# Forgetting attention with a spectral mode mix: attention matmuls padded to 128 rows, score blocks of one bank interleaved over four buffers

## The chip, the cores and the metric

One core of a Trainium2 chip. The metric is the device time of one execution in microseconds, the median of several executions; lower is better.

## The reference, cut to what matters

```python
# q, k, v: 8 batches x 8 heads x 576 x 64;  f: 8 x 8 x 576;  float32 in and out
scores = scale * q @ k^T                                # per batch and head, 576 x 576
decay  = cum[:, :, :, None] - cum[:, :, None, :]        # cum = cumsum(log f)
attn   = softmax(where(causal, -1e9, scores + decay))
x      = (attn @ v) laid out as [8, 576, 512]
X      = rfft(x, axis=1)[:, :64]                        # 64 modes
Y      = complex product of X[:, m] with w_r[m], w_i[m] # 64 pairs of 512 x 512 weights
u      = x + irfft(Y);   out = u + relu(u @ w_ch)
```

## The kernel before

Four stages follow one another: setup; attention, batch by batch, with the discrete Fourier transform of each batch; the 64 modes, whose 512 KB weight loads follow one another; output. The change touches attention and what its buffers are. In it, heads are taken in pairs; `S` is 576 and its five blocks have 128, 128, 128, 128 and 64 rows (`SBLK`).

```python
def emit_loads_and_casts(b):
    # ... qf, kf, vf float32 staging tiles, one buffer each; 15 loads per batch ...
                nc.sync.dma_start(dst[:ns, sc, :, :], t_dram[b, :, sc*128 : sc*128+ns, :]...)
    # ... cast by VectorE to qb, kb, vaug (bf16); the last block has 64 rows ...

def emit_qk_pair(b, g):                       # two heads, 2g and 2g + 1
    for sc in range(NSB):
        ns = SBLK[sc]
        nc.tensor.transpose(QTp[:, sc*128 : sc*128+ns], qb[:ns, sc, 2*g : 2*g+2, :]..., ident_bf[:ns, :ns])
        nc.tensor.transpose(KTp[...],                   kb[:ns, sc, 2*g : 2*g+2, :]..., ident_bf[:ns, :ns])
    nc.vector.tensor_copy(QTs[:, :], QTp[:, :])         # [128 = two heads x 64, S]
    nc.vector.tensor_copy(KTs[:, :], KTp[:, :])
    for hp in range(2):
        bp = hp * 64
        for jb in range(NSB):
            pscore = psA.tile([128, S], F32, ...)       # two banks; psA has two buffers
            for c0 in range(0, wj, 512):
                nc.tensor.matmul(pscore[:Mj, c0 : c0+n],
                    lhsT=KTs[bp : bp+64, s0 : s0+Mj], rhs=QTs[bp : bp+64, ...])   # 64 rows
            nc.scalar.activation(et[:Mj, :wj], pscore[:Mj, :wj], ACT.Exp, bias=..., scale=scale)
            nc.vector.tensor_tensor(et[:Mj, :Mj], et[:Mj, :Mj], trimask[:Mj, :Mj], ALU.mult)

def emit_dft_group(b, eb):                    # a transform: 5 matmuls, the last of 64 rows
    # ... pd[:, :] += x_b[:ns, sc, ...]^T @ bas[:ns, sc, ...]
    nc.vector.tensor_copy(XT[:, eb, :, :, b], pd...)    # XT is [128, NEB, NM, 2, B]

for b in range(B):
    emit_loads_and_casts(b)
    for g in range(H // 2):
        emit_qk_pair(b, g)
        # ... then 4 tail tasks of the batch before: value products (pav) and transforms (pd) ...
```

The softmax here doesn't subtract the row's maximum and nothing guards it: scores larger than these inputs give would overflow.

Of the kernel before, what the change touches and what calls it, by code (L numbers as in the profile page):

```python
# [10 lines left out]
F32 = mybir.dt.float32  # L11
# [12 lines left out]
def kernel(  # L24
# [28 lines left out]
    XT = xpool.tile([128, NEB, NM, 2, B], BF16, name="XT")  # L53
# [24 lines left out]
    wch = const.tile([128, NEB, D], BF16, name="wch")  # L78

# [116 lines left out]
    with ExitStack() as actx:  # L196
# [6 lines left out]
            tc.tile_pool(name="psA", bufs=2, space=bass.MemoryType.PSUM)  # L203
# [9 lines left out]
        per_batch = {}  # L213

        def emit_loads_and_casts(b):
# [3 lines left out]
            for t_dram, dst in ((q, qf), (k, kf), (v, vf)):  # L219
                for sc in range(NSB):  # L220
                    ns = SBLK[sc]
                    nc.sync.dma_start(  # L222
                        dst[:ns, sc, :, :],
                        t_dram[b, :, sc * 128 : sc * 128 + ns, :].rearrange(
                            "h p d -> p h d"
                        ),
                    )
            qb = qkbf.tile([128, NSB, H, Dh], BF16, tag="qb", name="qb")
            kb = qkbf.tile([128, NSB, H, Dh], BF16, tag="kb", name="kb")
            nc.vector.tensor_copy(qb[:, 0:4, :, :], qf[:, 0:4, :, :])  # L230
            nc.vector.tensor_copy(qb[:64, 4, :, :], qf[:64, 4, :, :])
            nc.vector.tensor_copy(kb[:, 0:4, :, :], kf[:, 0:4, :, :])  # L232
# [9 lines left out]
        def emit_qk_pair(b, g):  # L242
            st = per_batch[b]
            qb, kb = st["qb"], st["kb"]
            QTp = psT.tile([128, S], BF16, tag="tr", name="QTp")
            KTp = psT.tile([128, S], BF16, tag="tr", name="KTp")
            for sc in range(NSB):
                ns = SBLK[sc]
                nc.tensor.transpose(  # L249
                    QTp[:, sc * 128 : sc * 128 + ns],  # L250
                    qb[:ns, sc, 2 * g : 2 * g + 2, :].rearrange("p h d -> p (h d)"),
                    ident_bf[:ns, :ns],
                )
                nc.tensor.transpose(  # L254
                    KTp[:, sc * 128 : sc * 128 + ns],
                    kb[:ns, sc, 2 * g : 2 * g + 2, :].rearrange("p h d -> p (h d)"),
                    ident_bf[:ns, :ns],
                )
            QTs = qtkt.tile([128, S], BF16, tag="QTs", name="QTs")
            KTs = qtkt.tile([128, S], BF16, tag="KTs", name="KTs")  # L260
            nc.vector.tensor_copy(QTs[:, :], QTp[:, :])
            nc.vector.tensor_copy(KTs[:, :], KTp[:, :])
            for hp in range(2):
                h = 2 * g + hp
                bh = b * H + h
                bp = hp * 64
                for jb in range(NSB):
                    Mj = SBLK[jb]
                    s0 = jb * 128
                    wj = S - s0  # L270
                    pscore = psA.tile([128, S], F32, tag="sc", name="pscore")
                    for c0 in range(0, wj, 512):
                        n = min(512, wj - c0)
                        nc.tensor.matmul(  # L274
                            pscore[:Mj, c0 : c0 + n],
                            lhsT=KTs[bp : bp + 64, s0 : s0 + Mj],
                            rhs=QTs[bp : bp + 64, s0 + c0 : s0 + c0 + n],
# [3 lines left out]
                    et = epool.tile([128, wj], BF16, tag=f"e{jb}", name=f"et{jb}")  # L281
                    st["etiles"][(h, jb)] = et
                    nc.scalar.activation(  # L283
                        et[:Mj, :wj],
                        pscore[:Mj, :wj],
                        ACT.Exp,
                        bias=biasAll[:Mj, jb, bh : bh + 1],
                        scale=scale,
                    )
                    nc.vector.tensor_tensor(  # L290
                        et[:Mj, :Mj], et[:Mj, :Mj], trimask[:Mj, :Mj], ALU.mult
                    )
# [238 lines left out]
```

## Time and profile before

| | us |
|---|---|
| median of 6 runs first given | 716.82 (715.25 to 720.5) |
| median of all 16 runs of the comparison | 718.23 (715.25 to 720.5) |
| profiled span | 713.5 |
| to the first score matmul | 37.1 |
| attention, to the first mode matmul | 291.5 |
| modes / output | 318.5 / 66.4 |

Only one view is added here: the page's 40 equal slices of the span, each digit the busy share of an engine in tenths (9 is 90% or more); the last row is the TensorE clock, in tenths of full speed.

```profile
PE   0189999999998999899778752222222222227885
...
DVE  6356565656565656554222120000000000003454
ACT  2064646464545555461322320000000000003443
...
PEclk9999999999999999997999995555555555557998
```

Attention is slices 2 to 18, counted from 0: PE at eights and nines, VectorE (DVE) at fives and sixes, ScalarE (ACT) mostly at fours to sixes.

The clock entries of this trace hold two levels, 1.00 and 0.50, and all but the last are multiples of 3.41 us long; the shortest, at 323.93 us, is one such step. Below, warm is the level of 1.00 and cold that of 0.50; promotion is the change from cold to warm, demotion the change back; a window is one step of 3.41 us; a switch is where the next matmul has other rows or columns of the array.

### The profile page before, as it was taken

To read this page: it belongs to the slowest core of one execution; us is meant where nothing else is said; L and a number is where in the kernel's file an instruction comes from. 1 tells how busy PE (TensorE), PEld (TensorE's weight loads), DVE (VectorE), ACT (ScalarE), POOL (GpSimd) and SP (SyncE) were. 2 spreads that over 40 slices of the span, in tenths; PEclk is the share of its full clock that TensorE was granted. 3 is DMA by queue.
4 is the path that set the end of the run, shared out by engine and by line. 5 is a ranking of instruction groups with operands and counts; after the bars stand their busy time and mean duration, and the time that the engine had idled before them with its cause. 6 is when DMAs were issued, how large, how long until landed. Compare 5 with 4: busy or idle time off the path is not lost.

```text
span 713.5 us, 11166 instructions
## 1 busy us (share of the span) xinstructions
PE 452.9 (63%) x4412; PEld 253.4 (36%) x4428; DVE 264.5 (37%) x915; ACT 229.1 (32%) x478; POOL 98.5 (14%) x148
## 2 busy tenths in 40 slices
PE   0189999999998999899778752222222222227885
PEld 0035454545454544446444331111111111113332
DVE  6356565656565656554222120000000000003454
ACT  2064646464545555461322320000000000003443
POOL 3000000000000000002323232322323232210000
PEclk9999999999999999997999995555555555557998
DMA  9995536363645442004999999999999999993444
GB/s 194 212 213 108 114 71 129 68 131 70 116 85 112 88 94 41 1 1 76 204 207 206 207 206 206 206 206 206 206 206 206 207 206 207 206 207 84 158 164 148
DMA packets 186004, 106.78 MB, mean 150 GB/s; under 512 B 115232, under 2 KB 180768, under 8 KB 185952
## 3 DMA queue, kind: packets, MB, share of 16 engines
q0 software_dynamic: 67584, 67.12, 56.9%
q1 hardware_dynamic: 118368, 38.96, 25.7%
q8 instruction: 34, 0.56, 0.3%
q14 instruction: 18, 0.15, 0.1%
HBM read 163.73 MB, written 9.44 MB: 243 GB/s over the span
## 4 chain that ended last, share of the span: by engine, by line
DMA 44%; PE 37%; DVE 7%; ACT 5%; issue 4%; POOL 2%; SPq 1%; DVEq 0%; ACTq 0%; POOLq 0%
DMA wb<-in_moe_w_i_dram 38%; PE pscore L274 12%; PE pav L306 11%; ACT et L283 4%; DMA out_dram<-o_sb 4%; PE KTp L254 3%; PE pd L329 3%; PE QTp L249 3%; PE A L419 2%; POOL wb L409 2%; DVE o_sb L497 2%; DVE kb L232 2%; SPq L222 1%; DMA wch_f<-in_moe_w_ch_dram 1%; DMA kf<-in_k_dram 1%
## 5 line engine op out<-in xcount | busy, mean ns | idle before, releaser
L283 ACT ACTIVATE et<-pscore,biasAll 128x576 bf16<-128x576 f32 (+4 forms) x320 | 156.4, 524 | 142.1 <-PE pscore L274 137.2
L419 PE MATMUL A<-XT,wb 128*128 128x16 bf16 x2048 | 74.2, 174 | 189.8 <-DMA wb<-in_moe_w_r_dram 94.3
L274 PE MATMUL pscore<-QTs,KTs 64*128 64x512 bf16 (+5 forms) x384 | 128.3, 405 | 17.0 <-ACT et L283 14.5
L419 PEld LDWEIGHTS <-wb 128*128 128x128 bf16 x2048 | 63.2, 103 | 212.5 <-DMA wb<-in_moe_w_r_dram 106.7
L430 DVE TENSOR_TENSOR YT<-As 128x32 bf16<-128x32 f32 x64 | 19.2, 301 | 255.3 <-ACT As L427 255.3
L306 PE MATMUL pav<-vaug,et 128*128 128x65 bf16 (+2 forms) x960 | 97.0, 245 | 2.0 <-DVE x_all L315 0.2
L427 ACT COPY As<-A 128x128 f32<-128x128 f32 x64 | 17.0, 266 | 247.7 <-PE A L419 245.5
L290 DVE TENSOR_TENSOR et<-et,trimask 128x128 bf16<-128x128 bf16 (+1 forms) x320 | 64.6, 210 | 68.7 <-ACT et L283 66.3
L409 POOL DMA_DIRECT2D wb<-in_moe_w_r_dram x64 | 47.7, 745 | 282.8 <-PE A L419 271.2
L306 PEld LDWEIGHTS <-et 128*128 128x128 bf16 (+2 forms) x960 | 65.8, 130 | 57.7 <-issue 31.1
L274 PEld LDWEIGHTS <-KTs 64*128 64x128 bf16 (+1 forms) x384 | 38.2, 117 | 54.3 <-issue 40.8
L412 POOL DMA_DIRECT2D wb<-in_moe_w_i_dram x64 | 48.0, 750 | 1.8 <-issue 1.8
L398 PE MATMUL pxw<-wch,xT 128*128 128x512 bf16 (+1 forms) x148 | 42.4, 405 | 1.4 <-issue 0.6
L497 DVE SCALAR_TENSOR_TENSOR o_sb<-pz,u_sb 128x512 f32<-128x512 f32 (+1 forms) x40 | 27.5, 690 | 28.5 <-DMA out_dram<-o_sb 18.4
L239 POOL MEMSET vaug<- 128x40 bf16 x8 | 2.3, 282 | 250.3 <-PE pscore L274 119.2
L405 ACT CAST XW<-pxw 128x512 bf16<-128x512 f32 (+1 forms) x40 | 23.4, 585 | 38.7 <-PE pxw L398 36.4
L315 DVE TENSOR_TENSOR x_all<-pav,rcp 128x256 bf16<-128x256 f32 (+1 forms) x80 | 33.6, 420 | 0.6
L249 PE MATMUL QTp<-ident_bf,qb 128*128 128x128 bf16 (+1 forms) x160 | 26.1, 294 | 9.1 <-DVE qb L230 9.1
L254 PE MATMUL KTp<-ident_bf,kb 128*128 128x128 bf16 (+1 forms) x160 | 25.9, 292 | 7.5 <-DVE kb L232 7.5
L495 ACT CAST u_sb<-pu 128x512 bf16<-128x512 f32 (+1 forms) x40 | 23.4, 586 | 22.2 <-DVE o_sb L497 16.0
L329 PE MATMUL pd<-bas,x_all 128*128 128x128 bf16 (+1 forms) x160 | 24.5, 295 | 2.6 <-ACT et L283 2.3
L336 DVE CAST XT<-pd 128x128 bf16<-128x128 f32 x32 | 23.1, 730 | 4.9 <-PE pd L329 3.9
(90 smaller groups left out, 341.0 us busy)
## 6 DMA issues: line engine op xcount, KB each, us to landing
wb<-in_moe_w_r_dram POOLq DMA_DIRECT2D x64, 512.0 KB, 11.8
wb<-in_moe_w_i_dram POOLq DMA_DIRECT2D x64, 512.0 KB, 13.6
qf<-in_q_dram SPq DMA_DIRECT2D x32, 256.0 KB, 4.5
kf<-in_k_dram SPq DMA_DIRECT2D x32, 256.0 KB, 4.6
vf<-in_v_dram SPq DMA_DIRECT2D x32, 256.0 KB, 4.6
out_dram<-o_sb SPq DMA_DIRECT2D x32, 256.0 KB, 2.0
wch_f<-in_moe_w_ch_dram SPq DMA_DIRECT2D x1, 1024.0 KB, 5.8
qf<-in_q_dram SPq DMA_DIRECT2D x8, 128.0 KB, 4.5
```

The source lines that it names most:

```text
L249: nc.tensor.transpose(QTp[:, sc * 128 : sc * 128 + ns], qb[:ns, sc, 2 * g : 2 * g + 2, :].rearrange("p h d -> p (h d)"), ident_bf[:ns, :ns],)
L254: nc.tensor.transpose(KTp[:, sc * 128 : sc * 128 + ns], kb[:ns, sc, 2 * g : 2 * g + 2, :].rearrange("p h d -> p (h d)"), ident_bf[:ns, :ns],)
L274: nc.tensor.matmul(pscore[:Mj, c0 : c0 + n], lhsT=KTs[bp : bp + 64, s0 : s0 + Mj], rhs=QTs[bp : bp + 64, s0 + c0 : s0 + c0 + n], start=Tru ...
L283: nc.scalar.activation(et[:Mj, :wj], pscore[:Mj, :wj], ACT.Exp, bias=biasAll[:Mj, jb, bh : bh + 1], scale=scale,)
L290: nc.vector.tensor_tensor(et[:Mj, :Mj], et[:Mj, :Mj], trimask[:Mj, :Mj], ALU.mult)
L306: nc.tensor.matmul(pav[:Ms, hq, :], lhsT=et[:Mj, ccol : ccol + Ms], rhs=vaug[:Mj, h, jb, :], start=(jb == 0), stop=(jb == sb),)
L329: nc.tensor.matmul(pd[:, :], lhsT=x_b[:ns, sc, eb * 128 : (eb + 1) * 128], rhs=bas[:ns, sc, :, :].rearrange("p m ri -> p (m ri)"), start=( ...
L398: nc.tensor.matmul(pxw[:Ms, :], lhsT=xT[:, eb, sb * 128 : sb * 128 + Ms], rhs=wch[:, eb, :], start=(eb == 0), stop=(eb == NEB - 1),)
L409: nc.gpsimd.dma_start(wb[:, 0, :, :], moe_w_r[m].rearrange("(dc p) e -> p dc e", p=128))
L412: nc.gpsimd.dma_start(wb[:, 1, :, :], moe_w_i[m].rearrange("(dc p) e -> p dc e", p=128))
L419: nc.tensor.matmul(A[:, t, ebx, :], lhsT=wb[:, t, dc, ebx * 128 : (ebx + 1) * 128], rhs=XT[:, dc, m, :, :].rearrange("p ri b -> p (ri b)") ...
L497: nc.vector.scalar_tensor_tensor(o_sb[:Ms, :], pz[:Ms, :], 0.0, u_sb[:Ms, :], ALU.max, ALU.add)
```

## The change

Its intent: full use of the array's rows in attention, and scores that reach ScalarE without holes. It has these parts.

1. K of each head stands in its own copy `KTz` with zeros in the other head's 64 rows, so that a score matmul contracts over 128 rows; the last blocks of q, k and x are zero padded, so transposes and transforms have 128 rows.
2. Score blocks have at most 512 columns (one bank), in four buffers instead of two of two banks; the two heads of a pair alternate; the next pair's transposes and the last batch's tails are put between the score blocks.
3. `XT` has its modes contiguous, so the transform's eviction writes contiguous elements.
4. The v loads of batches 1 to 7 are issued on GpSimd's queue.

```diff
-    XT = xpool.tile([128, NEB, NM, 2, B], BF16, name="XT")
+    XT = xpool.tile([128, NEB, B, NM, 2], BF16, name="XT")
+    KTz = const.tile([128, 2, 2, S], BF16, name="KTz")
-            tc.tile_pool(name="psA", bufs=2, space=bass.MemoryType.PSUM)
+            tc.tile_pool(name="psA", bufs=4, space=bass.MemoryType.PSUM)
+        nc.vector.memset(KTz[64:128, :, 0, :], 0.0)
+        nc.vector.memset(KTz[0:64, :, 1, :], 0.0)
-                    nc.sync.dma_start(
+                    (nc.gpsimd if t_dram is v and b > 0 else nc.sync).dma_start(
+            nc.gpsimd.memset(qb[64:128, 4, :, :], 0.0)      # and kb, x_all
 # transposes: [:ns, ...] and ident_bf[:ns, :ns] become [:, ...] and ident_bf[:, :]
-            nc.vector.tensor_copy(KTs[:, :], KTp[:, :])
+                nc.vector.tensor_copy(KTz[0:64, slot, 0, :], KTp[0:64, :S])
+                nc.vector.tensor_copy(KTz[64:128, slot, 1, :], KTp[64:128, :S])
-            for hp in range(2):
-                for jb in range(NSB):
-                    pscore = psA.tile([128, S], F32, tag="sc", name="pscore")
+            for jb in range(NSB):
+                for c0 in range(0, wj, 512):
+                    for hp in range(2):
+                        pscore = psA.tile([128, 512], F32, tag="sc", name="pscore")
                         nc.tensor.matmul(
-                            lhsT=KTs[bp : bp + 64, s0 : s0 + Mj],
-                            rhs=QTs[bp : bp + 64, s0 + c0 : s0 + c0 + n],
+                            lhsT=KTz[:, g % 2, hp, s0 : s0 + Mj],
+                            rhs=QTs[:, s0 + c0 : s0 + c0 + n],
+                    # ... then the two activations and masks ...
+                if fillers:
+                    fillers.pop(0)()     # next pair's transposes, old tails
 # transform: x_b[:ns, ...], bas[:ns, ...] become x_b[:, ...], bas[:, ...]
-                XT[:, eb, :, :, b],
+                XT[:, eb, b, :, :],
 # mode matmul
-                            rhs=XT[:, dc, m, :, :].rearrange("p ri b -> p (ri b)"),
+                            rhs=_strided(XT[:, dc, 0, m, 0:1], [[1, 2], [NM * 2, B]]),
```

More of the change, by code (lines that the diff above doesn't have):

```diff
@@ L229, in emit_loads_and_casts @@
             kb = qkbf.tile([128, NSB, H, Dh], BF16, tag="kb", name="kb")
+            nc.gpsimd.memset(qb[64:128, 4, :, :], 0.0)
             nc.vector.tensor_copy(qb[:, 0:4, :, :], qf[:, 0:4, :, :])
             nc.vector.tensor_copy(qb[:64, 4, :, :], qf[:64, 4, :, :])
+            nc.gpsimd.memset(kb[64:128, 4, :, :], 0.0)
             nc.vector.tensor_copy(kb[:, 0:4, :, :], kf[:, 0:4, :, :])
@@ L240, in emit_loads_and_casts, with transpose_items @@
             per_batch[b] = dict(qb=qb, kb=kb, vaug=vaug, etiles={})
-        def emit_qk_pair(b, g):
+        def transpose_items(b, g):
             st = per_batch[b]
             qb, kb = st["qb"], st["kb"]
-            QTp = psT.tile([128, S], BF16, tag="tr", name="QTp")
-            KTp = psT.tile([128, S], BF16, tag="tr", name="KTp")
+            QTp = psT.tile([128, NSB * 128], BF16, tag="tr", name="QTp")
+            KTp = psT.tile([128, NSB * 128], BF16, tag="tr", name="KTp")
+            QTs = qtkt.tile([128, S], BF16, tag="QTs", name="QTs")
+            slot = g % 2
+            st[("QTs", g)] = QTs
+            items = []
@@ L247, in emit_qk_pair @@
             for sc in range(NSB):
                 ns = SBLK[sc]
-                nc.tensor.transpose(
-                    QTp[:, sc * 128 : sc * 128 + ns],
-                    qb[:ns, sc, 2 * g : 2 * g + 2, :].rearrange("p h d -> p (h d)"),
-                    ident_bf[:ns, :ns],
-                )
-                nc.tensor.transpose(
-                    KTp[:, sc * 128 : sc * 128 + ns],
-                    kb[:ns, sc, 2 * g : 2 * g + 2, :].rearrange("p h d -> p (h d)"),
-                    ident_bf[:ns, :ns],
-                )
@@ L259, in emit_qk_pair, with trq @@
-            QTs = qtkt.tile([128, S], BF16, tag="QTs", name="QTs")
-            KTs = qtkt.tile([128, S], BF16, tag="KTs", name="KTs")
-            nc.vector.tensor_copy(QTs[:, :], QTp[:, :])
-            nc.vector.tensor_copy(KTs[:, :], KTp[:, :])
+                def trq(sc=sc, ns=ns):
+                    nc.tensor.transpose(
+                        QTp[:, sc * 128 : sc * 128 + 128],
+                        qb[:, sc, 2 * g : 2 * g + 2, :].rearrange("p h d -> p (h d)"),
+                        ident_bf[:, :],
+                    )
@@ new lines, in trk, with evict @@
+                def trk(sc=sc, ns=ns):
+                    nc.tensor.transpose(
+                        KTp[:, sc * 128 : sc * 128 + 128],
+                        kb[:, sc, 2 * g : 2 * g + 2, :].rearrange("p h d -> p (h d)"),
+                        ident_bf[:, :],
+                    )
+                items.append(trq)
+                items.append(trk)
+            def evict():
+                nc.vector.tensor_copy(QTs[:, :], QTp[:, :S])
+                nc.vector.tensor_copy(KTz[0:64, slot, 0, :], KTp[0:64, :S])
+                nc.vector.tensor_copy(KTz[64:128, slot, 1, :], KTp[64:128, :S])
@@ L263, in emit_qk_pair @@
+            items.append(evict)
+            return items
+        def emit_qk_pair(b, g, fillers):
+            st = per_batch[b]
+            QTs = st[("QTs", g)]
+            ets = {}
             for hp in range(2):
                 h = 2 * g + hp
-                bh = b * H + h
-                bp = hp * 64
                 for jb in range(NSB):
-                    Mj = SBLK[jb]
-                    s0 = jb * 128
-                    wj = S - s0
-                    pscore = psA.tile([128, S], F32, tag="sc", name="pscore")
-                    for c0 in range(0, wj, 512):
-                        n = min(512, wj - c0)
+                    wj = S - jb * 128
+                    et = epool.tile([128, wj], BF16, tag=f"e{jb}", name=f"et{jb}")
+                    st["etiles"][(h, jb)] = et
+                    ets[(hp, jb)] = et
+            for jb in range(NSB):
+                Mj = SBLK[jb]
+                s0 = jb * 128
+                wj = S - s0
+                for c0 in range(0, wj, 512):
+                    n = min(512, wj - c0)
+                    pss = []
+                    for hp in range(2):
+                        pscore = psA.tile([128, 512], F32, tag="sc", name="pscore")
@@ L274, in emit_qk_pair @@
                         nc.tensor.matmul(
-                            pscore[:Mj, c0 : c0 + n],
-                            lhsT=KTs[bp : bp + 64, s0 : s0 + Mj],
-                            rhs=QTs[bp : bp + 64, s0 + c0 : s0 + c0 + n],
+                            pscore[:Mj, 0:n],
+                            lhsT=KTz[:, g % 2, hp, s0 : s0 + Mj],
+                            rhs=QTs[:, s0 + c0 : s0 + c0 + n],
                             start=True,
@@ L280, in emit_qk_pair @@
                         )
-                    et = epool.tile([128, wj], BF16, tag=f"e{jb}", name=f"et{jb}")
-                    st["etiles"][(h, jb)] = et
-                    nc.scalar.activation(
-                        et[:Mj, :wj],
-                        pscore[:Mj, :wj],
-                        ACT.Exp,
-                        bias=biasAll[:Mj, jb, bh : bh + 1],
-                        scale=scale,
-                    )
-                    nc.vector.tensor_tensor(
-                        et[:Mj, :Mj], et[:Mj, :Mj], trimask[:Mj, :Mj], ALU.mult
-                    )
+                        pss.append(pscore)
+                    for hp in range(2):
+                        h = 2 * g + hp
+                        bh = b * H + h
+                        et = ets[(hp, jb)]
+                        nc.scalar.activation(
+                            et[:Mj, c0 : c0 + n],
+                            pss[hp][:Mj, 0:n],
+                            ACT.Exp,
+                            bias=biasAll[:Mj, jb, bh : bh + 1],
+                            scale=scale,
+                        )
+                        if c0 == 0:
+                            nc.vector.tensor_tensor(
+                                et[:Mj, :Mj], et[:Mj, :Mj], trimask[:Mj, :Mj], ALU.mult
+                            )
+                if fillers:
+                    fillers.pop(0)()
         def emit_av_group(b, hh, sb):
@@ L325, in emit_dft_group @@
             x_b = x_all[:, b, :, :]
-            pd = psA.tile([128, 128], F32, tag="sc", name="pd")
+            pd = psA.tile([128, 512], F32, tag="sc", name="pd")
             for sc in range(NSB):
@@ L329, in emit_dft_group @@
                 nc.tensor.matmul(
-                    pd[:, :],
-                    lhsT=x_b[:ns, sc, eb * 128 : (eb + 1) * 128],
-                    rhs=bas[:ns, sc, :, :].rearrange("p m ri -> p (m ri)"),
+                    pd[:, 0:128],
+                    lhsT=x_b[:, sc, eb * 128 : (eb + 1) * 128],
+                    rhs=bas[:, sc, :, :].rearrange("p m ri -> p (m ri)"),
                     start=(sc == 0),
@@ L336, in emit_dft_group, with tail_items @@
             nc.vector.tensor_copy(
-                XT[:, eb, :, :, b],
-                pd[:, :].rearrange("p (m ri) -> p m ri", ri=2),
+                XT[:, eb, b, :, :],
+                pd[:, 0:128].rearrange("p (m ri) -> p m ri", ri=2),
             )
-        def tail_tasks(b):
+        def tail_items(b):
             tasks = []
@@ L344, in tail_tasks @@
                 for sb in range(NSB):
-                    tasks.append(("av", b, hh, sb))
+                    tasks.append(lambda b=b, hh=hh, sb=sb: emit_av_group(b, hh, sb))
             for eb in range(NEB):
-                tasks.append(("dft", b, eb))
+                tasks.append(lambda b=b, eb=eb: emit_dft_group(b, eb))
             return tasks
-        def run_task(t):
-            if t[0] == "av":
-                emit_av_group(t[1], t[2], t[3])
-            else:
-                emit_dft_group(t[1], t[2])
-        pending = []
-        for b in range(B):
-            emit_loads_and_casts(b)
-            for g in range(H // 2):
-                emit_qk_pair(b, g)
-                n_take = ((g + 1) * len(pending)) // (H // 2) if False else 4
-                for _ in range(min(len(pending), n_take)):
-                    run_task(pending.pop(0))
-            while pending:
-                run_task(pending.pop(0))
-            pending = tail_tasks(b)
-        while pending:
-            run_task(pending.pop(0))
+        nc.vector.memset(x_all[64:128, :, 4, :], 0.0)
+        pairs = [(b, g) for b in range(B) for g in range(H // 2)]
+        tails = []
+        for i, (b, g) in enumerate(pairs):
+            if i == 0:
+                emit_loads_and_casts(b)
+                for it in transpose_items(b, 0):
+                    it()
+            fillers = []
+            if i + 1 < len(pairs):
+                nb, ng = pairs[i + 1]
+                if ng == 0:
+                    emit_loads_and_casts(nb)
+                fillers.extend(transpose_items(nb, ng))
+            ntake = 4
+            for _ in range(min(ntake, len(tails))):
+                fillers.append(tails.pop(0))
+            emit_qk_pair(b, g, fillers)
+            for it in fillers:
+                it()
+            if g == H // 2 - 1:
+                while tails:
+                    tails.pop(0)()
+                tails = tail_items(b)
+        for it in tails:
+            it()
     with ExitStack() as bctx:
```

## The prediction

> **What bounds the kernel now.** I read the page's 40 slices first, then the chain, then the stretches of each stage. The chain's line by line shares:
>
> ```profile
> DMA wb<-in_moe_w_i_dram 38%; PE pscore L274 12%; PE pav L306 11%; ACT et L283 4%; DMA out_dram<-o_sb 4%; PE KTp L254 3%; PE pd L329 3%; PE QTp L249 3%; PE A L419 2%; POOL wb L409 2%; DVE o_sb L497 2%; DVE kb L232 2%; SPq L222 1%; DMA wch_f<-in_moe_w_ch_dram 1%; DMA kf<-in_k_dram 1%
> ```
>
> There are four stages: setup to the first score matmul at 37.1 us, attention to the first mode matmul at 328.6, the 64 modes (bound by the weight DMA, which holds 205 to 207 GB/s) to 648, output to 713. The change touches attention; a microsecond taken there moves the mode stage forward by a microsecond, because that stage needs the transforms of every batch and prefetches only three modes. Attention is 291.5 us, 36.5 per batch. Busy times of it, and of the mode stage (PE, PEld, DVE, ACT, POOL, clock, DMA share, GB/s):
>
> ```profile
> 72.00:288.00 216.00, 198.27 (x1342) 106.72 (x1342) 131.34 (x465) 117.20 (x240) 1.66 (x6) 1.00 0.48 92
> ...
> 430.00:645.00 215.00, 50.03 (x1344) 42.41 (x1344) 18.60 (x84) 11.17 (x42) 59.21 (x80) 0.50 1.24 205
> ```
>
> PE is busy 92% of attention, VectorE 61%, ScalarE 54%; ScalarE waits for PE (96.9 us), PE hardly for ScalarE (10.5):
>
> ```profile
> ACT et L283 <- PE pscore L274: 96.9, 85, 8.1
> ...
> PE pscore L274 <- ACT et L283: 10.5, 27, 0.5
> ```
>
> So attention is PE-bound. The clock of 1.00 above is not to be believed. The trace's clock records begin only at 323.93 us, with a grant of full speed; before that there is nothing, and the page prints nothing as full speed. The timeline across that moment:
>
> ```profile
> 320.59 1.59 PE L329 MATMUL pd<-bas,x_all 128*128 128x128 bf16 x10
> 322.12 1.56 PE L306 MATMUL pav<-vaug,et 128*128 128x65 bf16 x25
> 323.48 0.76 PE L329 MATMUL pd<-bas,x_all 128*128 128x128 bf16 x5
> 324.17 1.62 PE L306 MATMUL pav<-vaug,et 128*64 128x65 bf16 x20
> 325.73 1.05 PE L329 MATMUL pd<-bas,x_all 128*128 128x128 bf16 x10
> ```
>
> The same ten transform matmuls take 1.59 us before and 1.05 after. The groups by form say it again, first for 72 to 288, then for 324.2 to 327.5:
>
> ```profile
> L329 PE MATMUL pd<-bas,x_all 128*128 128x128 bf16 x96 | 14.5, 306 | 1.9 <-ACT et L283 1.9
> ```
>
> ```profile
> L329 PE MATMUL pd<-bas,x_all 128*128 128x128 bf16 x12 | 1.2, 224 | 0.4 <-DVE XT L336 0.4
> ```
>
> Start to start, the 25 value matmuls at 322.12 are (1.56-0.25)/24 = 55 ns apart for 65 columns, 0.84 ns a column; transform matmuls of 128 columns are 107 ns apart before 323.9 and 55 after. **All of attention runs at half clock.**
>
> I split the 216 us by start-to-start distance in the unmerged timeline (1,340 records). Streaming at 1.2 columns per ns: 137 us. Distance in excess of it where the next matmul has the same rows and columns of the array: 1 ns. Where rows or columns differ (64*128 after 128*128 and so on): 428 times, 130 ns each, 56 us. Long waits: 22 us. Per batch: 22.8 streaming, 9.3 switches, 3.7 waits.
>
> [...]
>
> **The change, part by part.**
>
> Padding to 128 rows (KTz, qb, kb, x_all). It removes every 64-row matmul of scores, transposes and transforms. Left are the column switches of the last score block (about 8 a batch) and of the value product's last block (18): 26 of 74. Saved at half clock: 48 x 130 ns = 6.2 us per batch. Streaming grows a little: 12,800 score + 7,800 value + 5,120 transpose + 2,560 transform columns = 28,280, 23.6 us cold, 11.8 warm.
>
> The clock. Weighting each window's streamed columns by rows/128, windows of this trace that promoted (outside transposes) had 0.63 to 0.87 of capacity, those of attention that did not at most 0.70; warm windows of 0.36 and more mostly held, 0.35 and less were demoted. This threshold is my estimate, from the trace's start times. With full rows a batch offers 23.3 us of weighted streaming in some 28: 0.8, so promotion. Warm, 11.7 in 25 is 0.47: mostly held, with cold windows now and then.
>
> ScalarE. The 576 activation is split into 512 and 64. By the rows below, +688-741+308 = 255 ns per head (688 interpolated), 2.0 us per batch: 19.5 becomes 21.5.
>
> ```profile
> L283 ACT ACTIVATE et<-pscore,biasAll 128x576 bf16<-128x576 f32 x48 | 35.6, 741 | 74.3 <-PE pscore L274 73.4 <-DVE x_all L315 0.8
> L283 ACT ACTIVATE et<-pscore,biasAll 128x448 bf16<-128x448 f32 x48 | 30.1, 627 | 0.0
> ...
> L283 ACT ACTIVATE et<-pscore,biasAll 64x64 bf16<-64x64 f32 x48 | 14.8, 308 | 5.6 <-PE pscore L274 4.0
> ```
>
> VectorE. The K eviction becomes two of 64 partitions, same 576 elements: 4 x 451 ns more. XT's new order lets the transform's eviction write 128 contiguous elements:[...] about 280, for 728: 4 x 450 ns less. Sum zero: 21.9 us per batch stays.
>
> ```profile
> L336 DVE CAST XT<-pd 128x128 bf16<-128x128 f32 x24 | 17.5, 728 | 3.7 <-PE pd L329 2.9
> ...
> L262 DVE COPY KTs<-KTp 128x576 bf16<-128x576 bf16 x23 | 10.4, 451 | 11.3 <-PE KTp L254 10.2 <-PE QTp L249 1.1
> ```
>
> Four one-bank score buffers for two of two banks, heads interleaved, next transposes and old tails as fillers: it shortens the 3.7 us of waits and lets PE feed ScalarE without long holes. The v loads on GpSimd take 5 of 15 issues (about 1.07 us each in the chain) off the sync queue; loads are hidden already (DMA share 0.48), so nothing, also at 25 us a batch (0.7). New memsets: x_all 4,096 elements and KTz 2 x 1,152[...]; +1 us. The mode matmul now reads its 16 columns in steps of 256 bytes; the stage uses PE 50 of 215 us, so nothing but at its ends.
>
> **Sum.** Warm, PE needs 11.8 + 26 x about 0.1 = 14 to 15 us per batch and the floor is VectorE 21.9 and ScalarE 21.5. Both near 87%[...]: 25 us. First batch, no tails, partly cold: 23. Last tails exposed, warm: 7. 23 + 7x25 + 7 = 205, plus 1 at the start: 291.5-206 = 85.5 saved, 716.8-85.5 = 631. I say 631.
>
> **Rivals.** (1) The clock stays cold. For it: before, 290 us of a 92% busy PE never promoted; transposes may not count as activity. Then PE stays the bound: 23.6 + 3.6 + 1.5 waits = 28.7; 24 + 7x28.7 + 10 = 235, so about 661. (2) VectorE and ScalarE pack to their floor: 22.3 a batch, 21 + 7x22.3 + 7 = 184, about 610. Against it: trimask and evictions wait on one another; the eviction of the next K stands in line on VectorE, and a late one stalls PE and ScalarE together. (3) It is given back in the mode stage by slow strided reads. Even 80 ns for 26 makes 32 matmuls 2.6 us, under the 5 us of DMA per mode; exposed at most at the first mode and the last, 4 us: 635. (4) The engines are bound by loads: needs 18 us of DMA per batch, under 25; little.
>
> **Range and chances.** Rivals 2 and 1 set the ends: 608 to 661. All of them are faster by over 7%, so faster 0.95; the rest is for a wrong schedule or for loads that hold up a batch.
>
> **What would show it.** Right: transform matmuls about 55 ns apart (mean near 224) in the middle of attention; clock records there; no 64*128 matmuls in scores, transposes, transforms; PE busy under 75%, VectorE and ScalarE near 85%; XT eviction near 280 ns; attention about 205 us; mode stage at 205 GB/s and as long as before. Wrong: matmuls still 107 ns apart (rival 1); XT eviction still 700; a mode stage longer by over 5 us; ScalarE waiting on DMA.

## The result, and the profile after

| | before | after |
|---|---|---|
| median us | 718.23 (16 runs) | 611.67 (609.53 to 612.76, 8 runs) |
| profiled span | 713.5 | 609.1 |
| start, to the first score matmul | 37.1 | 38.2 |
| first batch (its first exponential to that of the next) | 35.4 | 30.1 |
| batches 1 to 7, to the last exponential | 247.3 | 147.8 |
| last tails, to the first mode matmul | 8.1 | 7.0 |
| attention in all | 291.5 | 185.6 |
| modes | 318.5 | 318.4 |
| output | 66.4 | 66.9 |

(The three attention rows begin 0.7 us after the first score matmul, so they sum to 0.7 less than the whole.) The ratio is 0.852, 95% interval 0.8504 to 0.8536. Here and below a ratio compares the fast runs of the two kernels in the same rounds, so it is not quite the ratio of the medians quoted. The gain of 106 us is attention's; nothing was given back later. All outputs are right.

The slices of the kernel after, to be laid beside those of before:

```profile
PE   0156888988988998888772222222222222249885
...
DVE  8357899999999862123120000000000000015453
ACT  2047589988987832332330000000000000015443
...
PEclk9998699999999988898995555555555555559999
```

Attention now ends in slice 14, and VectorE stands at nines in it. This clock row is a record: the trace's clock entries begin at 40.4 us and show full speed to 57.4, half to 71.1 (the 6), then full speed without a break to 224.7. The chain that ended last has lost PE's share to the weight loads, which were as long before:

```profile
DMA wb<-in_moe_w_i_dram 45%; PE pav L343 6%; DMA out_dram<-o_sb 6%; PE pscore L305 4%; ACT et L317 4%; PE A L463 3%; POOL wb L453 3%; DVE o_sb L541 2%; DVE et L325 2%; DMA vf<-in_v_dram 2%; PE pxw L442 1%; DMA qf<-in_q_dram 1%; DVE x_all L352 1%; DVE vaug L241 1%; PE pd L366 1%
```

Busy times by stretch (PE, PEld, VectorE, ScalarE, GpSimd, clock, DMA share, GB/s): five whole batches, all of the steady part, and the mode stage.

```profile
89.30:197.20 107.90, 93.72 (x1085) 63.65 (x1084) 100.61 (x402) 92.39 (x241) 22.34 (x33) 1.00 0.77 144
...
72.00:217.00 145.00, 127.81 (x1485) 86.98 (x1482) 133.75 (x545) 126.03 (x330) 28.11 (x40) 1.00 0.68 128
235.00:542.00 307.00, 125.23 (x2194) 84.80 (x2204) 37.68 (x148) 37.26 (x97) 85.49 (x116) 0.62 1.23 205
```

VectorE is busy 93% of the five batches (100.61 of 107.90), ScalarE 86%, PE 87%. PE's figure counts each matmul from start to modelled end; by start-to-start distances PE's work is about 17.8 of 21.6 us per batch, so PE is no longer the bound. The modes move 205 GB/s, as before.

PE's groups by form, 72 to 217 us: the transform, 306 ns at half clock before, is

```profile
L366 PE MATMUL pd<-bas,x_all 128*128 128x128 bf16 x140 | 10.5, 219 | 0.7
```

That is the warm figure of the old kernel (224) all through attention, and the tile field shows no 64-row transform left. The groups of VectorE and of ScalarE, 89 to 197 us (count, busy us, mean ns, idle before):

```profile
L325 DVE TENSOR_TENSOR et<-et,trimask 128x128 bf16<-128x128 bf16 x160 | 29.5, 212 | 1.8 <-ACT et L317 0.8
...
L280 DVE COPY KTz<-KTp 64x576 bf16<-64x576 bf16 x20 | 9.2, 461 | 0.6
L279 DVE COPY KTz<-KTp 64x576 bf16<-64x576 bf16 x20 | 8.8, 441 | 0.0
...
L373 DVE CAST XT<-pd 128x128 bf16<-128x128 f32 x20 | 5.1, 280 | 0.2
```

```profile
L317 ACT ACTIVATE et<-pscore,biasAll 128x512 bf16<-128x512 f32 x41 | 26.1, 690 | 12.9 <-PE pscore L305 12.7 <-DVE et L325 0.2
L317 ACT ACTIVATE et<-pscore,biasAll 128x448 bf16<-128x448 f32 x40 | 23.7, 652 | 0.9 <-PE pscore L305 0.8
...
L317 ACT ACTIVATE et<-pscore,biasAll 128x64 bf16<-128x64 f32 x40 | 10.5, 325 | 0.0
```

The transform's eviction fell from 728 to 280 ns. Note 29.5 us of busy time for 160 masks of 212 ns, which would be 33.9: an instruction that follows at once starts before the one ahead has ended. This matters below. The waits of ScalarE and PE in the same stretch (total us, times, longest):

```profile
ACT et L317 <- PE pscore L305: 15.4, 21, 1.6
```

```profile
PE pscore L305 <- ACT et L317: 7.5, 29, 0.4
```

ScalarE's wait for PE fell from 96.9 us in 216 to 15.4 in 108. Last, the first batch, in its timeline:

```profile
57.97 1.23 DVE L241 CAST vaug<-vf 128x2048 bf16<-128x2048 f32 x1 [4.07 <-DMA vf<-in_v_dram]
...
68.98 1.27 ACT L317 ACTIVATE et<-pscore,biasAll 128x512 bf16<-128x512 f32 x2 [7.05 <-PE QTp L261]
```

VectorE sat idle 4 us for a load, the casts that stand behind it came late, and ScalarE idled 7 us before the second batch. This points to loads as the bound of the first batch; a run below tests it.

### The profile page after: what moved, and what is told of

It is laid out like the page before. It is cut to its first block, busy times and chain, and to the rows that moved or that the text cites. A ratio compares the mean times of both kernels' runs of the same rounds, so it can differ in the third digit from the quotient of the medians.

```text
span 609.1 us, 11331 instructions
## 1 busy us (share of the span) xinstructions
PE 353.6 (58%) x4411; PEld 224.7 (37%) x4428; DVE 256.0 (42%) x950; ACT 220.3 (36%) x542; POOL 138.6 (23%) x199
## 4 chain that ended last, share of the span: by engine, by line
DMA 53%; PE 17%; DVE 12%; ACT 4%; POOL 3%; issue 2%; SPq 0%; DVEq 0%; ACTq 0%
DMA wb<-in_moe_w_i_dram 45%; PE pav L343 6%; DMA out_dram<-o_sb 6%; PE pscore L305 4%; ACT et L317 4%; PE A L463 3%; POOL wb L453 3%; DVE o_sb L541 2%; DVE et L325 2%; DMA vf<-in_v_dram 2%; PE pxw L442 1%; DMA qf<-in_q_dram 1%; DVE x_all L352 1%; DVE vaug L241 1%; PE pd L366 1%
## 5 line engine op out<-in xcount | busy, mean ns | idle before, releaser
L317 ACT ACTIVATE et<-pscore,biasAll 128x320 bf16<-128x320 f32 (+5 forms) x384 | 147.7, 499 | 48.0 <-PE pscore L305 40.2
L474 DVE TENSOR_TENSOR YT<-As 128x32 bf16<-128x32 f32 x64 | 19.3, 302 | 254.9 <-ACT As L471 254.9
L305 PE MATMUL pscore<-QTs,KTz 128*128 128x512 bf16 (+1 forms) x383 | 89.6, 282 | 15.7 <-ACT et L317 11.6
L343 PE MATMUL pav<-vaug,et 128*128 128x65 bf16 (+2 forms) x960 | 66.4, 200 | 6.6 <-DVE x_all L352 5.9
L343 PEld LDWEIGHTS <-et 128*128 128x128 bf16 (+2 forms) x960 | 50.7, 103 | 29.2 <-DVE x_all L352 7.5
L305 PEld LDWEIGHTS <-KTz 128*128 128x128 bf16 (+1 forms) x384 | 35.8, 100 | 29.6 <-issue 13.2
L226 POOL DMA_DIRECT2D vf<-in_v_dram x35 | 30.4, 878 | 65.2 <-DMA qf<-in_q_dram 35.3
L539 ACT CAST u_sb<-pu 128x512 bf16<-128x512 f32 (+1 forms) x40 | 23.4, 586 | 22.1 <-DVE o_sb L541 13.8
L261 PE MATMUL QTp<-ident_bf,qb 128*128 128x128 bf16 x160 | 19.2, 233 | 13.9 <-DVE qb L235 11.2
L437 DVE COPY xT<-ptr 128x576 bf16<-128x576 bf16 x32 | 14.4, 464 | 22.8 <-PE ptr L432 22.7
L268 PE MATMUL KTp<-ident_bf,kb 128*128 128x128 bf16 x160 | 19.6, 231 | 6.1 <-DVE kb L238 5.2
L477 DVE TENSOR_TENSOR YT<-As 128x32 bf16<-128x32 f32 x64 | 21.6, 337 | 0.0
## 6 DMA issues: line engine op xcount, KB each, us to landing
wb<-in_moe_w_r_dram POOLq DMA_DIRECT2D x64, 512.0 KB, 11.7
```

The costliest lines, as they stand in the source:

```text
L226: (nc.gpsimd if t_dram is v and b > 0 else nc.sync).dma_start(dst[:ns, sc, :, :], t_dram[b, :, sc * 128 : sc * 128 + ns, :].rearrange("h p ...
L305: nc.tensor.matmul(pscore[:Mj, 0:n], lhsT=KTz[:, g % 2, hp, s0 : s0 + Mj], rhs=QTs[:, s0 + c0 : s0 + c0 + n], start=True, stop=True,)
L317: nc.scalar.activation(et[:Mj, c0 : c0 + n], pss[hp][:Mj, 0:n], ACT.Exp, bias=biasAll[:Mj, jb, bh : bh + 1], scale=scale,)
L343: nc.tensor.matmul(pav[:Ms, hq, :], lhsT=et[:Mj, ccol : ccol + Ms], rhs=vaug[:Mj, h, jb, :], start=(jb == 0), stop=(jb == sb),)
L539: nc.scalar.copy(u_sb[:Ms, :], pu[:Ms, :])
```

## The experiments

The main theory, **clock**: padding lets the array be granted full clock, and that is most of the gain. Its rival, **structure**: the four buffers, the interleave and the order take away waits, and padding saves only switches. Every ratio is to the kernel before in the same rounds.

### Padding alone

The kernel before with part 1 only: `KTz`, zero pads, 128-row transposes, scores and transforms; order, buffers, `XT` and load queues as before.

```diff
-                            lhsT=KTs[bp : bp + 64, s0 : s0 + Mj],
-                            rhs=QTs[bp : bp + 64, s0 + c0 : s0 + c0 + n],
+                            lhsT=KTz[:, g % 2, hp, s0 : s0 + Mj],
+                            rhs=QTs[:, s0 + c0 : s0 + c0 + n],
 # and the full-row transposes and transforms, as in the change
```

> The kernel before with the padding to 128 rows alone (scores, transposes, transforms); order of heads, score buffers, XT layout and v loads as before. Theory clock (full rows promote the clock, the rest matters little): transform matmuls 55 ns apart in attention, batches of 22 to 26 us, total 610 to 650. Rival switches[...]: clock stays at half, 36.5 - 6.2 = 30.3 us a batch, total about 667. Rival structure (fillers and four score buffers bring the gain): total about 690 to 710.

Measured: 681.1 us (675.31 to 682.91), ratio 0.9491 (0.9441 to 0.9541): a third of the gain. Its page's clock row:

```profile
PEclk9978787886565656858999955555555555557999
```

The clock swings: promoted, held for some windows, demoted again. By its records it is at full speed in 37% of attention, and a batch takes 29 to 35 us. So padding does get the clock promoted, as the clock theory has it, but alone it does not hold it. None of the three expectations was met exactly.

### Everything but padding

The kernel after with all padding removed (scores, transposes and transforms of 64 rows where they were so before; one K copy; no zero fills).

```diff
-                            lhsT=KTz[:, g % 2, hp, s0 : s0 + Mj],
-                            rhs=QTs[:, s0 + c0 : s0 + c0 + n],
+                            lhsT=KTz[hp*64 : hp*64+64, g % 2, s0 : s0 + Mj],
+                            rhs=QTs[hp*64 : hp*64+64, s0 + c0 : s0 + c0 + n],
 # and the ns-row transposes and transforms of the kernel before
```

> The changed kernel with all of its padding taken out (scores, transposes and transforms of 64 rows as before), but its order, buffers, XT layout and v loads kept. Clock: row-weighted activity stays under 0.70 of a cold window, no promotion, 32 to 36 us a batch, total 680 to 715. Structure: most of the gain stays, total 615 to 650.

Measured: 680.2 us, ratio 0.9494 (0.9469 to 0.9518). There is no clock record before 289.7 us, and the matmuls are spaced as at half clock: the nine below are (0.68-0.25)/8 = 54 ns apart for 65 columns.

```profile
136.72 0.68 PE L338 MATMUL pav<-vaug,et 128*128 128x65 bf16 x9
```

A batch takes 31.0 us. Counted by columns, PE streams 22.1 us per batch and waits 1.1 (3.7 before). But the 22.1 count some time twice: about six times a batch two score matmuls of 64 rows start 3 to 6 ns apart, which the kernel before never shows, and in all about 3 us of score columns per batch stream under one another. So the structure is worth about 36 us by itself, at half clock: of some 5.5 us per batch, about 2.5 are waits and 3 are this overlap of half-row matmuls, which padding gives up. The structure theory, which expected 615 to 650, falls.

By their ratios to some 717 us, padding alone takes 36 us, everything else 36, both 106. **The remaining 34 us come only with both**: padding supplies the activity, and the even feed holds the clock that it earns. (Since the overlap is lost with padding, this is the least that the two are worth to one another.)

### Scores of 64 rows, the rest padded

```diff
-                            lhsT=KTz[:, g % 2, hp, s0 : s0 + Mj],
-                            rhs=QTs[:, s0 + c0 : s0 + c0 + n],
+                            lhsT=KTz[hp*64 : hp*64+64, g % 2, s0 : s0 + Mj],
+                            rhs=QTs[hp*64 : hp*64+64, s0 + c0 : s0 + c0 + n],
```

> The changed kernel with only its score matmuls back at 64 rows (transposes and transforms stay padded). If the activity that promotes the clock is weighted by rows: 21,900 weighted columns a batch are 18.2 us of about 33 us, 0.55, mostly no promotion, total 670 to 700. If rows do not count, only streamed columns: 0.7 to 0.85 of the window, promotion, total 612 to 630. The two heads now follow one another in different halves of the rows and may overlap, which no theory above sizes.

Measured: 672.99 us, ratio 0.9381 (0.932 to 0.9441). The clock row:

```profile
PEclk9985555558555555679999755555555555558998
```

Full speed in 7% of attention only. **So it is the padding of the scores that the clock needs.** Why is less clear. The columns are the same as in the kernel after, but three things change with the rows of the scores: the rows themselves, the switches between 64 and 128 rows (130 ns each in the kernel before), and the overlap of the two heads (some nine pairs a batch start 3 to 6 ns apart). From the start times I counted, for each 3.4 us step of the clock records, the share of it in which columns streamed. Windows of this run that were not promoted had 0.50 to 1.03 with overlapping columns counted twice, 0.49 to 0.78 by time, and at most 0.74 weighted by rows/128. In the run of padding alone, promoted windows had 0.73 to 0.87 weighted (and some of up to 0.76 were not promoted), and 0.72 to 0.83 by time. At promotion, time and rows are thus too close to tell apart; the next run helps. The threshold, about 0.75, is an estimate from these counts, and not a sharp one: in the kernel after, the window that ended at 71.1 us was promoted at 0.67.

### A burst of full matmuls in the kernel before

16 dummy matmuls of 128 rows and 512 columns ahead of each batch, results unused; the other expectation was that promotion would last.

```diff
             for g in range(H // 2):
+                if g == 0:
+                    emit_burst()      # 16 x matmul(pb[:, 0:512], ident_bf, bas[:, 0:4])
                 emit_qk_pair(b, g)
```

> The kernel before with 16 more full matmuls of 512 columns in front of each batch (3.4 us of streaming warm, 6.8 cold, results unused). Clock: each burst fills a window and promotes; warm, weighted activity is about 0.34 to 0.4 of a window against a demotion level near 0.355, so attention is warm for some of each batch, and the kernel gets faster by added work: 620 to 700. Switches or structure: the burst only adds, 8 x 3.4 to 6.8 us, total 745 to 772.

Measured: 723.63 us, ratio 1.0101 (1.0072 to 1.013). Both expectations missed. The clock row of the page, and the bursts themselves as a group (72 to 288 us):

```profile
PEclk9855757575657575755899895555555555556999
```

```profile
L297 PE MATMUL pburst<-bas,ident_bf 128*128 128x512 bf16 x81 | 23.8, 457 | 0.0
```

Each burst brings some 10 us of full clock, then 27 us of half; the batch takes 37.6 us with the burst, 36.5 before. The burst nearly pays for itself, and the clock does not stay: promotion alone is not enough, the work after it must be dense enough to hold it.

These windows show that rows count. No matmuls overlap in them, yet in attention six of the seven that lost full speed had columns streaming for 0.41 to 0.48 of the time, by rows only 0.25 to 0.36; the kernel after held every window from 71.1 us on, down to 0.38.

### Two score buffers instead of four

```diff
-            tc.tile_pool(name="psA", bufs=4, space=bass.MemoryType.PSUM)
+            tc.tile_pool(name="psA", bufs=2, space=bass.MemoryType.PSUM)
```

> The changed kernel with two score buffers of one bank for four. If four buffers are what keeps PE's activity even enough to hold the clock: windows under 0.37 of capacity come back, the clock swings as in the padding-only kernel, total 640 to 690. If the order of heads and fillers holds it: 612 to 622.

Measured: 647.71 us, ratio 0.9026; 36 us more than the kernel after. A batch takes 26.8 us and the clock row has dips:

```profile
PEclk9987878899798996999889555555555555558999
```

Full speed in 79% of batches 1 to 6, against 98% with four buffers. In the runs with padding, windows at full speed with a weighted share of 0.38 or more held and those of 0.37 or less were demoted (estimates, from the same counts; the two overlap at the second digit). The kernel after has 0.38 to 0.72 in attention, and all windows from 71.1 us on held. The buffers are thus part of what makes the feed even. How much of the 36 us is the clock and how much is plain waiting was not separated.

### The old XT layout in the kernel after

```diff
-    XT = xpool.tile([128, NEB, B, NM, 2], BF16, name="XT")
+    XT = xpool.tile([128, NEB, NM, 2, B], BF16, name="XT")
 # eviction and mode matmul accordingly
```

> The changed kernel with only XT back in its old order: the transform's eviction writes 128 elements 16 bytes apart (about 730 to 790 ns for 280), and the mode matmul reads contiguous columns. If VectorE is the bound of attention (it is busy 20.4 of 22 us a batch): 4 x 0.45 to 0.5 = 1.8 to 2.0 us more a batch, total 624 to 628. If it is not, or if the strided read of the mode matmuls costs as much: 608 to 614.

Measured: 620.95 us (620.58 to 621.82), ratio 0.8658 (0.8637 to 0.8679): 9.3 us more than the kernel after. The eviction, and the busy times of its five batches 2 to 6:

```profile
L373 DVE CAST XT<-pd 128x128 bf16<-128x128 f32 x20 | 13.2, 791 | 0.2
```

```profile
90.70:204.70 114.00, 94.61 (x1084) 64.57 (x1082) 107.17 (x402) 94.13 (x241) 22.33 (x33) 0.97 0.72 135
```

VectorE's busy time rose by 1.3 us per batch (107.17 - 100.61 over 5) and the batch by 1.2 (22.8 for 21.6). It would have been 2.0 if each eviction's 511 extra ns stood alone; when the next instruction follows at once it started on average some 420 ns after the eviction's start, against 202 in the kernel after. The batch follows VectorE almost one for one. The rival is the clock, which fell to half twice here, for 3.4 us each; but batches 3 and 5, which have no such window, also took 23.0 to 23.1 us for 21.8. The mode stage is 318.4 us with either layout, though the mode matmul's median is 174 ns with the old one and 192 with the new. In the kernel after, its group on the page:

```profile
L463 PE MATMUL A<-XT,wb 128*128 128x16 bf16 x2048 | 82.4, 192 | 181.3 <-DMA wb<-in_moe_w_r_dram 92.3
```

PE waits for weights 181 us there. The slower read hides under the weight loads.

### The v loads back on the sync queue

```diff
-                    (nc.gpsimd if t_dram is v and b > 0 else nc.sync).dma_start(
+                    nc.sync.dma_start(
```

> The changed kernel with the v loads of all batches back on the sync queue. My prediction gave this part nothing: 608 to 616. Rival: 15 issues of about 1.1 us are 17 us of the queue per batch of 21 us, and loads come late: 618 to 640, with VectorE and PE waiting for loads after the first batch.

Measured: 623.4 us (622.9 to 624.3), ratio 0.8693 (0.8672 to 0.8713): 11.7 us more. Batches take 24 to 26 us, all but the last; the first takes 24.4, less than the 30.1 of the kernel after. The loads are not late: k of the batch shown was issued from 110.8 us on. At its boundary:

```profile
134.21 1.23 DVE L238 CAST kb<-kf 128x2048 bf16<-128x2048 f32 x1
...
137.94 0.69 ACT L317 ACTIVATE et<-pscore,biasAll 128x512 bf16<-128x512 f32 x1 [5.35 <-PE pscore L305]
```

The cast of K comes late among VectorE's instructions, at 134.21 us, behind the old batch's value tails; transposes, evictions and scores follow it, and ScalarE idles 5.35 us. The same place in the kernel after:

```profile
130.80 3.56 ACT L317 ACTIVATE et<-pscore,biasAll 128x512 bf16<-128x512 f32 x8 [1.56 <-PE pscore L305]
```

The two traces differ in the order of instructions on two engines: 416 of VectorE's 950 and about 1,430 of PE's 4,411 stand elsewhere, none of ScalarE's 542. So moving an issue from one queue to another changed the order in which the instructions were laid down, and most of the 11.7 us is put down to that order. A part is the clock: it fell to half for two windows in each of batches 3 and 6, which took 25.6 to 25.7 us where 1, 2, 4 and 5 took 24.7 to 24.9, so about 2 us. That the loads' own transfer took no part is argued from their times, not shown by a run.

### v cast in the load

v is loaded by GpSimd's queue straight into the bf16 tile, so VectorE has two casts fewer per batch.

```diff
-            vf = stg.tile([128, NSB, H, Dh], F32, tag="vf", name="vf")
+                nc.gpsimd.dma_start(vaug[:ns, :, sc, 0:Dh], v[b, :, sc*128 : sc*128+ns, :]...)
-            nc.vector.tensor_copy(vaug[:, :, 0:4, 0:Dh], vf[:, 0:4, :, :]...)   # and the last block
```

> The changed kernel with v loaded by GpSimd's DMA straight into the bf16 tile (the DMA casts), so the two v casts (1.21 + 0.41 us a batch) leave VectorE. VectorE-bound: up to 1.6 us a batch, 8 to 12 in all, total 598 to 604. If ScalarE (18.5 of 22 us) or the loads are the bound: 608 to 614; if the 128-byte pieces slow the loads: over 615.

Measured: 611.44 us, ratio 0.8522 (0.8501 to 0.8544): the same as the kernel after. The same five batches:

```profile
90.50:195.30 104.80, 93.57 (x1094) 64.31 (x1092) 95.13 (x391) 92.53 (x240) 32.62 (x38) 1.00 1.00 124
```

The DMA share is 1.00 for 0.77 in the kernel after, at 124 GB/s for 144, so these loads keep the DMA engines busy longer; the total does not show it. VectorE 19.0 us per batch for 20.1, the batch 21.0 for 21.6; over all seven batches 20.8 for 21.1. Half of VectorE's relief, or less, reaches the batch. The loads' new order puts the first exponential at 49.3 us (38.9 in the kernel after), but the second batch starts at 69.4, for 69.0, so the start as a whole gained nothing. With the old layout's run: VectorE is the nearest bound, and ScalarE, at 88%, stands close behind. How the last 1.5 to 2 us of a batch divide between the two stays open.

### An earlier first batch

Two changes to the kernel after. The pool of the exponentials is opened ahead of the staging pool, so the staging tiles no longer lie over the setup's tiles, for which the sync queue waited. And the first three modes' weights, issued at 5 to 9 us and landing by 24.1, just ahead of the first q load, are held until batch 4 (then batch 7) by a tiny write that depends on that batch's `vaug`.

```diff
+        epool = actx.enter_context(tc.tile_pool(name="epool", bufs=16))
         stg = actx.enter_context(tc.tile_pool(name="stg", bufs=1))
-        epool = actx.enter_context(tc.tile_pool(name="epool", bufs=16))
             wb = wpool.tile([128, 2, NEB, D], BF16, tag="wb", name="wb")
+            if m < 3:
+                nc.gpsimd.tensor_copy(wb[0:1, 0:2, 0, 0:1],
+                    per_batch[4]["vaug"][0:1, 0:2, 0, Dh : Dh + 1])   # [7] in the second
```

The wait that this removes, in the kernel after (the sync queue's own waits, 0 to 69 us):

```profile
SPq L226 <- DVE BI L150: 16.5, 1, 16.5
```

> The changed kernel with the loads ordered anew: the pool of score tiles is opened first, so that the q, k, v staging tiles no longer lie where the setup's tiles lay (the first q load waited 16.5 us for them), and the first three mode weights are not loaded at the start but after batch 4's v tile (they took DMA time while batches 0 and 1 waited for data). Theory for the first 69 us of the changed kernel: bound by loads (DMA share 1.1, 200 to 206 GB/s, VectorE idle 4.1 us for v, batch 0 takes 30 us for 21). Then first score at 24 to 30 us instead of 38, batch 1 at 46 to 54 instead of 69, total 590 to 600. Rival (setup or the clock holds batch 0): 606 to 612.

Measured with batch 4: 610.58 us, ratio 0.8503 (0.8475 to 0.8531). The second batch starts at 51.2 us, 17.8 earlier, and batch 4 takes 35.9 us: the weights now lie between its loads, and VectorE waits 7.1 us for q there:

```profile
DVE qb L235 <- DMA qf<-in_q_dram: 7.1, 1, 7.1
```

> As x9_after_early, but the first three mode weights wait for the last batch's v tile instead of batch 4's. In x9_after_early batch 1 began at 51 us (18 earlier than in the changed kernel) and batch 4 took 35.9 us for 22 while the weights came in between its loads. Theory loads: the stretch after batch 7's loads moves nothing today, so nothing is delayed, the 14 to 18 us stay: total 590 to 597. Rival (the gain at the start was given back by something other than these weights): 605 to 612.

Measured with batch 7: **595.09 us** (593.8 to 596.67), ratio 0.8303 (0.8281 to 0.8326). The first mode matmul is at 207.0 us, 16.8 earlier, and the mode stage takes 318.9. So the start was bound by when the loads came, for 17 us: the first exponential is 11.8 us earlier (27.1 for 38.9), and the first batch takes 24.1 us for 30.1. How much each of the two changes gave was not separated.

### The odd head's mask on GpSimd

The batch 4 version above, with half of the mask products moved to GpSimd.

```diff
-                            nc.vector.tensor_tensor(
+                            (nc.gpsimd if hp else nc.vector).tensor_tensor(
                                 et[:Mj, :Mj], et[:Mj, :Mj], trimask[:Mj, :Mj], ALU.mult
```

> The run x9_after_early with the causal mask of the odd head moved from VectorE to GpSimd. If VectorE is the bound of attention: 20 x 0.21 = 4.2 us a batch leave it, the bound becomes ScalarE at 18.5 to 20, so 1 to 2 us a batch and 8 to 14 us below x9_after_early. If GpSimd's slower multiply[...] takes it back: the same as x9_after_early or slower.

Measured: 608.49 us, ratio 0.8475 (0.8454 to 0.8496): no gain that can be told from its base. (The base is a poor one: both runs have weights among batch 4's loads, and full speed in only 78 to 80% of batches 1 to 6.) Groups, 146 to 200 us:

```profile
L325 POOL TENSOR_TENSOR et<-et,trimask 128x128 bf16<-128x128 bf16 x40 | 21.2, 538 | 13.9 <-ACT et L317 13.6
...
L325 DVE TENSOR_TENSOR et<-et,trimask 128x128 bf16<-128x128 bf16 x39 | 10.9, 284 | 0.9 <-ACT et L317 0.8
```

VectorE's own masks became slower, 284 ns for 212, while its copies of K and Q kept their 440 to 460 ns. What slowed them is not shown by any run. ScalarE's queue was busy 87% here as well.

### Both together

The batch 7 version with v cast in the load.

> x11_early_last with v cast in the DMA as in x7_after_vcast (there batches took 20.7 to 21.3 us for 21.7 to 22.4, and the gain went into a first score 10 us later, behind v's and the weights' loads). With q and k first: 4 to 6 us below x11_early_last, 585 to 592. If the 128-byte pieces hold up the loads: above it.

Measured: **592.79 us** (590.68 to 594.92), ratio 0.8264 (0.8237 to 0.8291), just outside the 585 to 592 expected. It is the fastest version found; its interval overlaps that of the version without the cast, so the cast's share is not sure.

## Why the prediction was right or wrong, step by step

Predicted 631 (608 to 661), measured 611.67: in the range, the direction right, the mechanism right in the main, 19 us too slow.

- **"All of attention runs at half clock": right.** The transform matmul went from 306 to 219 ns, and clock records now exist from 40.4 us on.
- **"With full rows ... promotion": right, and incomplete.** Padding of the scores is needed (672.99 without it), but the prediction named padding alone as the cause. Padding alone gave 681.1 with a swinging clock; the buffers and interleave, which the prediction put down to waits only, were needed to hold it.
- **"Warm, ... mostly held, with cold windows now and then": nearly.** From 71.1 to 224.7 us there was none. The estimate of demotion (0.35) was near what the runs show (0.37); that of promotion (0.63 to 0.70) was low for most windows (about 0.75).
- **"transposes may not count as activity" (rival 1): not borne out.** In the run of padding alone, with transposes left out of the count, promoted windows had 0.25 to 0.85 and those not promoted 0.26 to 0.72, without order; counted, 0.73 and more against at most 0.76.
- **Switches, 26 left per batch: right**, 28 at 123 ns. PE's need, "14 to 15", was too small: 11.4 streaming, 3.5 switches and 2.9 of shorter gaps (17 ns per matmul in the mean, 4 in the median) make 17.8. It did not bind, but the sign "PE busy under 75%" failed: 87%.
- **XT's eviction about 280 ns: right**, 280 for the 728 before. The prediction's figure was the author's estimate; no trace before the change shows a contiguous eviction of this form. In the run with the old layout it was worth 9.3 us, because VectorE is the nearest bound.
- **The new memsets, without effect on the sum.** They took 2.8 us on VectorE (1.77 and twice 0.54): the trace shows them as uint32, with half the elements.
- **"Both near 87%", so 25 us a batch: the term that was mis-sized.** Batches 1 to 7 took 147.8 us, not 175. The shares were near (VectorE 93%, ScalarE 86% in five batches); the sums under them were not. The prediction took 21.9 and 21.5 us from busy times of a kernel in which these engines were half idle. Measured over whole batches, instruction durations add up to 24.8 us on VectorE and 24.1 on ScalarE, but their busy time is 20.1 and 18.5: back to back, a 512-wide activation that lasts 688 ns is followed by the next after 576, and a mask of 212 after about 136. ScalarE's durations did rise, by 3.1 us (2.0 predicted), and its busy time fell, by 1.1. 20.1/0.93 is the 21.6 us of those batches. The range's lower end, rival 2, named a packing to 22.3 us; the batches went below it for this reason. That its total for attention, 184, is almost the 184.9 measured is luck: its first batch of 21 was 9 us too short, its seven others 8 us too long.
- **"First batch, no tails, partly cold: 23": wrong.** 30.1 us. It is bound by loads: in the run that moves them it takes 24.1, and starts 11.8 us earlier. The prediction had looked at the DMA share of attention's middle only (0.48); in the first batch before the change it was 0.88, hidden behind a PE that was busy for 33.0 of 36.1 us.
- **"loads are hidden already ... so nothing": wrong** for the v loads. They are worth 11.7 us, most of it put down to the order they cause.
- **Start +1, last tails 7, mode stage unchanged: right** (+1.1, 7.0, 318.4 for 318.5).

The sum: 23 + 175 + 7 = 205 was predicted, 30.1 + 147.8 + 7.0 = 184.9 measured. The batches' 27.2 us too much outweigh the first batch's 7.1 too little. That the result lies in the range is partly luck: with the first batch of 23 us that was predicted it would have been near 604.6, under the lower end of 608.

## What to carry to other kernels

When a busy array's matmuls lie twice as far apart as its fastest ones, look first whether the clock has any record at all, then at how many rows the matmuls use: here half-empty rows cost the clock as well as the rows (scores of 64 rows: full speed in 7% of attention, 672.99 us for 611.67). A floor worked out from busy times of a half-idle engine was too high here (21.9 us per batch on VectorE, 20.1 measured); take the distance between starts of instructions that follow one another at once. And when the middle of a kernel gets faster, work the first batch out anew, since loads that it used to hide can come into the open (here 30.1 us, and 24.1 with the loads moved).
